# Attention and two mixture layers on one core: a weight guard by magnitude and floor, column steps with pointer scalars, and a new order of all operations

## The chip, the cores and the metric

The kernel runs on one core of a Trainium2 chip. Its time is the device time of one execution in microseconds (us), the median over several executions. A core has five engines that matter here: TensorE (PE, matrix products, with a separate weight load PEld), VectorE (DVE), ScalarE (ACT), GpSimd (POOL) and the queue engine SyncE (SP), which issues the DMA transfers. Each engine works through its own list of instructions in a fixed order and waits, on semaphores, for what an instruction needs.

## The reference

Three layers follow each other. Only the shapes matter for the time, and the 64-bit weights of the second layer, which are the subject of the change.

```python
# 1. attention: B=4 batches, H=8 heads, 512 local + 32 global positions, head size 64
s_ll = where(|i - j| <= 32, scale * q_l @ k_l.T, -1e9)      # local: a band
a_l  = softmax(concat([scale * q_l @ k_g.T, s_ll]))          # and all global keys
out_l = a_l @ concat([v_g, v_l]);  out_g = softmax(scale * q_g @ k_all.T) @ v_all
# 2. x: 2304 tokens x 512.  w_in 512 x 1024 and w_out 1024 x 512 are scaled in NumPy
#    by a float64 scalar and so come in as 64-bit floats
h = x @ w_in;  solu = h * softmax(h)
ln = (solu - mean) / sqrt(var + 1e-6) * g_ln;   x2 = ln @ w_out
# 3. soft mixture of 8 experts with 4 slots each
logits = x2 @ phi;  slot_in = softmax(logits, axis=0).T @ x2
slot_out[e] = relu(slot_in[e] @ w1[e]) @ w2[e];  out = softmax(logits, axis=1) @ slot_out
```

## The kernel before

**Attention.** Tokens are worked on in 16 local tiles of 128 and in 4 global tiles. A local tile has matrix products of queries and keys (L710), a VectorE step that adds the mask and takes the row maximum (L718, output tile `E`), exponentials on ScalarE (L723), transposes on TensorE (L740), copies (L742), products with v (L755), a scaling on VectorE (L762) and a VectorE transpose (L766) into `xp`, the input tile of the next layer. The global tiles have the same steps on other lines: maxima at L795 to L798, sums and reciprocal at L809 and L810.

**Second layer.** There are 17 dense tiles. Each needs its input split into a high part (ScalarE, L859) and a low part (GpSimd subtraction, L860), and then takes 24 matrix products of 128x128 by 128x512 against the high and low parts of w_in (L868, output `h`; called h products below). Softmax and normalisation follow on VectorE and ScalarE (L883 to L932), with small steps on columns of 128x1: L884 takes the smaller of two negated maxima, L902 and L929 prepare mean and variance. `ln` (L911) goes through TensorE transposes (L921) into the product with w_out, which the kernel folds with phi into a small matrix `pb` (L664 to L682).

**Weights.** The 16 pieces of w_in and w_out (8 each, 128x512 numbers of 64 bits, tile `wst`) come in as pairs of 32-bit words. `load_weight` makes 32-bit floats of them: three integer steps on VectorE (L586 to L588, called bits below) join the words. A guard sets numbers that are too small for the format to zero. It has two forms. Form D (4 pieces of w_in): ScalarE squares the high word read as a float (L589), and VectorE compares and multiplies in one step (L593). Form P (12 pieces): the same square, then a comparison (L598) and a product (L599) on GpSimd. A w_in piece is then split into high (ScalarE, L610) and low (GpSimd, L611) parts.

**Third layer.** 47 units of w1 and w2 are loaded into slots as they come free; their products are at L1102 and L1143, and the combination and the stores follow at L1153 to L1180.

**What sets the order.** All operations are collected in a list, with an engine, an estimated duration and a priority each. `Schedule.run` walks a simulated time: whenever an engine is free it takes the ready operation with the lowest priority number, if the operation's buffers fit under the limits `CAPS` and `KEEP` for each kind of buffer (four `wst` buffers, for instance). The table `PRIORITY` has one number for each operation that is added to its priority. The result is a fixed order for each engine and for the DMA issues of SP (L533).

Of the kernel before, what the change touches and what calls it, by code (L numbers as in the profile page):

```python
# [103 lines left out]
class Fetch:  # L104
# [11 lines left out]
    def run(self, o, t, d):  # L116
        room = self.BLOCK - self.n % self.BLOCK
        if o.count >= room:
            self.entered = t + d * room / o.count
# [4 lines left out]
class Schedule:
# [40 lines left out]
    def run(self, on_start=None):  # L165
# [74 lines left out]
        while done < n:  # L240
            progress = False
            waits = []
            for e in engines:
# [115 lines left out]
CAPS = dict(h=10, p1=20, E=15, W=23, eT=29, lT=13, ln=15, q=17, u=9, v=25, wst=4, xhl=5, xp=3)  # L359
KEEP = dict(p1=3, E=3, W=2, eT=2, eg=6, lT=1, ln=5, mkx=22, q=1, u=3, v=7, w=10, wo=14, wst=3, xhl=4)  # L360
# [10 lines left out]
STAY = 16.0807791841  # L371
# [987 lines left out]
```

## Time and profile before

| what | value |
|---|---|
| time, median of 3 runs | 307.65 us (305.86 to 309.4) |
| profiled execution, own time | 306.45 us |
| its span in the trace | 304.7 us (1.75 us lie outside) |
| PE busy | 275.2 us (90%) |
| DVE busy | 203.8 us (67%) |
| ACT busy | 200.1 us (66%) |
| POOL busy | 112.8 us (37%) |
| moved by DMA | 73.0 MB, mean 240 GB/s |
| chain that ended last, by engine | PE 71%, DVE 11%, DMA 9%, ACT 4% |

Busy time is an average over the span, so the table alone does not say which engine decides at which time; a table by stretches of time does. The chain that ended last is found by going back from the last instruction to what released it, step by step.

### The profile page before, as it was taken

How to read it: one execution, taken by the hardware profiler on the slowest of the kernel's cores; microseconds unless marked ns; L12 is line 12 of the kernel's file. 1: busy time of each engine (PE TensorE's matmuls, PEld its weight loads, DVE VectorE, ACT ScalarE, POOL GpSimd, SP SyncE). 2: the span in 40 equal slices, each digit the busy share in tenths (PEclk: the TensorE clock that was granted, in tenths of full speed). 3: DMA queues.
4: the chain of work that ended last, by engine and by line, in shares of the span. 5: the costliest groups of instructions: out<-in, count | busy, mean ns of one | idle time of the engine just before them, and what ended most of it. 6: DMA issues, size and time to landing. Idle time of an engine off the chain costs nothing.

```text
span 304.7 us, 10894 instructions
## 1 busy us (share of the span) xinstructions
PE 275.2 (90%) x4374; PEld 205.6 (67%) x4374; DVE 203.8 (67%) x752; ACT 200.1 (66%) x655; POOL 112.8 (37%) x179
## 2 busy tenths in 40 slices
PE   1576888999999999999999999999999999998980
PEld 1455566786777887777788878877778775364660
DVE  0789899999997578967786777458577861020350
ACT  1766958798789699896898696557467772010250
POOL 0257759897663234243112253224231572000000
PEclk9999999999999999999999999999999999999996
DMA  6999999984202202398649408638545986999498
GB/s 209 407 404 413 409 409 404 408 334 134 86 2 74 71 12 71 81 400 303 230 142 356 137 2 306 225 94 267 197 162 198 339 291 212 357 375 360 132 307 266
DMA packets 31090, 72.99 MB, mean 240 GB/s; under 512 B 2624, under 2 KB 13376, under 8 KB 30656
## 3 DMA queue, kind: packets, MB, share of 16 engines
q1 hardware_dynamic: 30848, 72.17, 65.8%
q8 instruction: 34, 0.56, 0.8%
q10 hardware_dynamic: 192, 0.13, 0.2%
q14 instruction: 16, 0.13, 0.1%
HBM read 67.83 MB, written 4.46 MB: 237 GB/s over the span
## 4 chain that ended last, share of the span: by engine, by line
PE 71%; DVE 11%; DMA 9%; ACT 4%; SPq 2%; issue 2%; DVEq 0%; ACTq 0%
PE h L868 27%; PE p L921 5%; PE p L710 4%; PE p L1102 4%; PE p L755 4%; DMA v<-in_v 4%; PE p L740 4%; PE p L1143 3%; PE p L942 3%; DMA unit<-in_w 3%; PE p L987 3%; DMA q<-in_q 2%; PE p L831 2%; PE p L788 2%; SPq L533 2%
## 5 line engine op out<-in xcount | busy, mean ns | idle before, releaser
L868 PE MATMUL h<-w,xhl 128*128 128x512 f32 x408 | 106.1, 404 | 0.0
L868 PEld LDWEIGHTS h<-w,xhl 128*128 128x128 f32 x408 | 73.0, 189 | 15.7 <-issue 1.3
L723 ACT ACTIVATE E<-E,nmx 128x128 f32<-128x128 f32 x128 | 49.7, 393 | 8.9 <-DVE nmx L718 8.8
L718 DVE CUSTOM_DVE_ANT_0 E<-p,mkx 128x128 f32<-128x128 f32 x128 | 29.2, 284 | 8.6 <-PE p L710 8.2
L889 ACT ACTIVATE u<-h,st 128x512 f32<-128x512 f32 x34 | 23.2, 688 | 13.6 <-DVE st L884 13.6
L710 PE MATMUL p<-k,q 64*32 64x128 f32 x1024 | 22.3, 309 | 8.2 <-DMA q<-in_q 7.6
L883 DVE TENSOR_REDUCE st<-h 128x1 f32<-128x512 f32 x34 | 22.8, 683 | 10.0 <-PE h L868 9.7
L740 PE MATMUL p<-cs,E 128*128 128x128 f32 x128 | 21.9, 306 | 4.7 <-ACT E L723 4.7
L710 PEld LDWEIGHTS p<-k,q 64*32 64x32 f32 x1024 | 17.1, 118 | 13.1 <-DMA k<-in_k 7.9
L892 DVE SCALAR_TENSOR_TENSOR u<-h,u 128x512 f32<-128x512 f32 x34 | 22.9, 682 | 3.3 <-ACT u L889 3.1
L723 ACT ACTIVATION_READ_ACCUMULATOR E<-E,nmx 128x1 f32 x128 | 24.6, 192 | 0.0
L860 POOL TENSOR_TENSOR xhl<-xp,xhl 128x512 fp32r<-128x512 f32 x16 | 20.5, 1284 | 10.3 <-ACT xhl L859 10.1
L755 PE MATMUL p<-v,eT 128*32 128x64 f32 x1024 | 21.1, 234 | 3.2 <-DMA v<-in_v 2.0
L740 PEld LDWEIGHTS p<-cs,E 128*128 128x128 f32 x128 | 16.6, 154 | 9.2 <-ACT E L723 6.7
L755 PEld LDWEIGHTS p<-v,eT 128*32 128x32 f32 x1024 | 17.5, 118 | 7.5 <-issue 3.1
L598 POOL TENSOR_SCALAR wst<-wst 128x512 f32<-128x512 f32 x12 | 19.3, 1605 | 8.8 <-ACT wst L589 8.5
L926 ACT ACTIVATE lT<-p 128x512 f32<-128x512 f32 x33 | 18.8, 601 | 5.4 <-PE p L921 5.3
L742 ACT ACTIVATE eT<-p 128x512 f32<-128x512 f32 x32 | 18.8, 599 | 2.5 <-PE p L740 2.4
L927 ACT ACTIVATE u<-ln 128x1024 f32<-128x1024 f32 x17 | 18.0, 1060 | 3.6 <-DVE ln L911 3.6
L932 POOL TENSOR_TENSOR st<-st,eps 128x1 f32<-128x1 f32 x17 | 9.7, 569 | 25.9 <-DVE st L929 25.7
L921 PE MATMUL p<-cs,ln 128*128 128x128 f32 x136 | 19.1, 276 | 0.0
L728 POOL TENSOR_SCALAR r<-sm 128x8 f32<-128x8 f32 x16 | 4.3, 271 | 34.4 <-ACT E L723 34.0
(140 smaller groups left out, 556.8 us busy)
## 6 DMA issues: line engine op xcount, KB each, us to landing
unit<-in_w SPq DMA_DIRECT2D x47, 512.0 KB, 5.3
v<-in_v SPq DMA_DIRECT2D x28, 512.0 KB, 9.1
k<-in_k SPq DMA_DIRECT2D x3, 1536.0 KB, 8.8
k<-in_w SPq DMA_DIRECT2D x9, 512.0 KB, 5.0
wst<-in_w_out SPq DMA_DIRECT2D x8, 512.0 KB, 10.2
wst<-in_w_in SPq DMA_DIRECT2D x8, 512.0 KB, 10.4
out<-unit SPq DMA_DIRECT2D x8, 512.0 KB, 4.3
unit<-in_w SPq DMA_DIRECT2D x14, 256.0 KB, 7.3
```

The costliest lines, as they stand in the source:

```text
L598: op("Pool", 1680, lambda: nc.gpsimd.tensor_scalar(out=low(), in0=low(), scalar1=least * least, scalar2=None, op0=ALU.is_ge), (), (st,), d ...
L710: nc.tensor.matmul(out=sp[hh][32 * c : 32 * c + 32, a2 + i, :], lhsT=Q[rows, 4 * (a2 + i) + c, :], rhs=K[rows, c, s : s + 128], start=True ...
L718: nc.vector.tensor_tensor_reduce(out=E[:, hh, a, :], in0=sp[hh][:, a, :], in1=MK(mask_kind(4 * t + a)), scale=-SCALE, scalar=3.0e38, op0=A ...
L723: nc.scalar.activation(out=E[:, hh, a, :], in_=E[:, hh, a, :], func=AF.Exp, bias=nmx[:, hh, a : a + 1], scale=-1.0, accum_out=sm[:, hh, a ...
L740: nc.tensor.transpose(out=tp[:, a, :], in_=E[:, hh, a, :], identity=I())
L755: nc.tensor.matmul(out=av[32 * c : 32 * c + 32, hh, a, :], lhsT=eT[hh][:, a, 32 * c : 32 * c + 32], rhs=V[:, (g - 1) % 2, 64 * h : 64 * h ...
L860: op("Pool", 1250, lambda: nc.gpsimd.tensor_tensor(out=xl.ap, in0=X.ap, in1=xh.ap.bitcast(F32), op=ALU.subtract), (X, xh), (xl,))
L868: nc.tensor.matmul(out=hp[n].ap, lhsT=lhs[:, kt, :], rhs=rhs[kt][n].ap, start=(kt == 0 and lhs is xh and rhs is whi), stop=(kt == 3 and lh ...
L883: op("DVE", 602, lambda n=n: nc.vector.tensor_reduce(out=part(7 + n), in_=hp[n].ap, axis=AX.X, op=ALU.max, negate=True), (hp[n],), (col[7 ...
L889: op("ACT", 664, lambda n=n: nc.scalar.activation(out=u[:, n, :], in_=hp[n].ap, func=AF.Exp, bias=nm(), scale=1.0, accum_out=part(7 + n)), ...
L892: op("DVE", 613, lambda n=n: nc.vector.scalar_tensor_tensor(out=u[:, n, :], in0=hp[n].ap, scalar=1.0, in1=u[:, n, :], op0=ALU.mult, op1=AL ...
L921: nc.tensor.transpose(out=tp[:, n, :], in_=ln[:, f // 2, 128 * (f % 2) : 128 * (f % 2) + 128], identity=I())
```

## The change

1. All 16 pieces get one new guard, form M. ScalarE first takes the absolute value of the high word, read as a float, into the destination (L608 in the changed kernel). GpSimd takes the larger of that and a constant floor, in place (L609). Then the three bits steps run on VectorE (L598 to L600 in the changed kernel); the first of them now reads the floored word. The ScalarE and GpSimd steps therefore stand ahead of the bits, where the square, comparison and product stood behind them.
2. Four kinds of VectorE steps on columns are written as `tensor_scalar` with a column as pointer scalar, in place of two tensor inputs: the two steps L797 and L798 become one, and L809, L884 and L929 change their form.
3. The planner gets new constants (latency after a load, a delay behind slot-limited loads, a rule that keeps two marked GpSimd and VectorE operations apart), new limits `CAPS` and `KEEP`, and a new `PRIORITY` table, so the order of every engine is new. Line numbers move by 10 to 12.

```diff
-        def bits(last):
+        def bits(last, words):
             w = d.ap.bitcast(I32)
-            nc.vector.tensor_scalar(out=w, in0=st[:, :, 1], scalar1=3, scalar2=0x3FFFFFFF, op0=ALU.logical_shift_left, op1=ALU.bitwise_and)
+            nc.vector.tensor_scalar(out=w, in0=words, scalar1=3, scalar2=0x3FFFFFFF, op0=ALU.logical_shift_left, op1=ALU.bitwise_and)
...
-            op("DVE", 2050, lambda: bits(dst), (st,), (d, dst), dp=dp)
-            square()
-            op("Pool", 1680, lambda: nc.gpsimd.tensor_scalar(out=low(), in0=low(), scalar1=least * least, scalar2=None, op0=ALU.is_ge), (), (st,), dp=dp)
-            op("Pool", 1395, lambda: nc.gpsimd.tensor_tensor(out=dst.ap, in0=dst.ap, in1=low(), op=ALU.mult), (st,), (dst,), dp=dp)
+            op("ACT", 587, lambda: nc.scalar.activation(out=dst.ap, in_=high(), func=AF.Abs), (st,), (dst,), dp=dp)
+            op("Pool", 1680, lambda: nc.gpsimd.tensor_scalar(out=dst.ap, in0=dst.ap, scalar1=below, scalar2=None, op0=ALU.max), (), (dst,), dp=dp)
+            op("DVE", 2050, lambda: bits(dst, dst.ap.bitcast(I32)), (st,), (d, dst), dp=dp)
...
-                nc.vector.tensor_tensor(out=st[:, 2:3], in0=st[:, 0:1], in1=st[:, 1:2], op=ALU.max)
-                nc.vector.tensor_scalar(out=st[:, 2:3], in0=st[:, 2:3], scalar1=-SCALE, scalar2=None, op0=ALU.mult)
+                nc.vector.tensor_scalar(out=st[:, 2:3], in0=st[:, 0:1], scalar1=st[:, 1:2], scalar2=-SCALE, op0=ALU.max, op1=ALU.mult)
...
-                nc.vector.scalar_tensor_tensor(out=st[:, 5:6], in0=st[:, 3:4], scalar=1e-9, in1=st[:, 4:5], op0=ALU.add, op1=ALU.add)
+                nc.vector.tensor_scalar(out=st[:, 5:6], in0=st[:, 3:4], scalar1=1e-9, scalar2=st[:, 4:5], op0=ALU.add, op1=ALU.add)
...
-        op("DVE", 76, lambda: nc.vector.tensor_tensor(out=nm(), in0=part(7), in1=part(8), op=ALU.min), (col[7], col[8]), (col[0],))
+        op("DVE", 76, lambda: nc.vector.tensor_scalar(out=nm(), in0=part(7), scalar1=part(8), scalar2=None, op0=ALU.min), (col[7], col[8]), (col[0],))
...
-GUARD_IN, GUARD_OUT = "DP", "PP"
+GUARD_IN, GUARD_OUT = "MM", "MM"
...
-CAPS = dict(h=10, p1=20, E=15, W=23, eT=29, lT=13, ln=15, q=17, u=9, v=25, wst=4, xhl=5, xp=3)
-KEEP = dict(p1=3, E=3, W=2, eT=2, eg=6, lT=1, ln=5, mkx=22, q=1, u=3, v=7, w=10, wo=14, wst=3, xhl=4)
+CAPS = dict(h=9, p1=48, E=24, W=33, eT=35, lT=13, ln=17, q=8, u=15, v=27, wst=13, xhl=27, xp=17)
+KEEP = dict(p1=1, E=3, W=8, eT=2, lT=1, ln=3, mkx=26, q=3, u=2, v=1, w=7, wo=8, wst=4, xhl=4, xp=1)
...
-STAY = 16.0807791841
+STAY = 0.639248030591
```

**The order at three places.** The first is the start of SP's queue, so the order in which the first transfers are issued. `k` and `q` are keys and queries, `mkx` the mask, `cs` constants, `wst` a weight piece. Before:

```order
L533 DMA cs_70<-in_cst 128x256
L533 DMA k_72<-in_k 128x4x224
L533 DMA q_74<-in_q 128x512
L533 DMA mkx_76<-in_cst 128x512
L533 DMA k_72<-in_k 128x4x192
L533 DMA q_74<-in_q 128x512
L533 DMA wst_115<-in_w_out 128x1024
L533 DMA q_117<-in_q 128x512 x2
L533 DMA v_160<-in_v 128x1024
L533 DMA wst_176<-in_w_in 128x1024
```

In the changed kernel:

```order
L545 DMA mkx_70<-in_cst 128x512
L545 DMA k_72<-in_k 128x4x224
L545 DMA wst_74<-in_w_in 128x1024
L545 DMA q_76<-in_q 128x512
L545 DMA cs_78<-in_cst 128x256
L545 DMA wst_80<-in_w_in 128x1024
L545 DMA k_72<-in_k 128x4x192
L545 DMA wst_86<-in_w_in 128x1024
L545 DMA wst_90<-in_w_in 128x1024
L545 DMA q_76<-in_q 128x512
```

Four pieces of w_in moved ahead of the second query block; before, the first weight piece, one of w_out, stood behind it. All eight w_in pieces are issued within the first 11.9 MB of transfers, where it was 17.2 MB.

The second place is the start of VectorE. `p` is a scratch tile in PSUM, `W` a w_in piece, `E` the masked scores of a local tile. Before, from the end of the first local tile's rows on:

```order
L718 ISA E_82,nmx_120<-p_7_80,mkx_76 128x128
L718 ISA nmx_120 128x1
L586 TENSOR_SCALAR p_18_171<-wst_115 128x512
L587 SCALAR_TENSOR_TENSOR p_18_171<-wst_115,p_18_171 128x512
L588 SCALAR_TENSOR_TENSOR wo_172<-wst_115,p_18_171 128x512
L718 ISA E_125,nmx_191<-p_13_123,mkx_76 128x128
```

In the changed kernel, from the first row behind the clearing of a buffer on:

```order
L598 TENSOR_SCALAR p_13_92<-W_82 128x512
L599 SCALAR_TENSOR_TENSOR p_13_92<-wst_74,p_13_92 128x512
L600 SCALAR_TENSOR_TENSOR W_82<-wst_74,p_13_92 128x512
L598 TENSOR_SCALAR p_19_137<-W_88 128x512
L599 SCALAR_TENSOR_TENSOR p_19_137<-wst_80,p_19_137 128x512
L600 SCALAR_TENSOR_TENSOR W_88<-wst_80,p_19_137 128x512
L729 ISA E_99,nmx_182<-p_15_98,mkx_70 128x128
L729 ISA nmx_182 128x1
```

The bits of two w_in pieces moved ahead of the first local tile's rows (L729 is the old L718).

The third place is TensorE around its first h products. `xhl` is a split input tile, `w` a split piece of w_in. Before:

```order
L755 MATMUL p_89_550<-v_228,eT_434 32x64 x4
L755 MATMUL p_89_550<-v_412,eT_434 32x64 x8
L755 MATMUL p_89_550<-v_401,eT_434 32x64 x4
L868 MATMUL h_571<-w_498,xhl_399 128x512 x3
L868 MATMUL h_571<-w_495,xhl_399 128x512 x3
L740 MATMUL p_96_593<-cs_70,E_459 128x128 x4
```

In the changed kernel:

```order
L721 MATMUL p_63_385<-k_72,q_251 32x128
L721 MATMUL p_64_386<-k_72,q_251 32x128
L878 MATMUL h_69_430<-w_324,xhl_420 128x512 x3
L878 MATMUL h_69_430<-w_141,xhl_420 128x512 x3
L721 MATMUL p_73_457<-k_72,q_251 32x128
L721 MATMUL p_74_458<-k_72,q_251 32x128
```

The first h product moved from row 166 to row 113 of TensorE: it now stands behind the scores of three local tiles, where before it stood behind four and the scores of a global tile.

## Rows read from the trace of the kernel before

**Rows 1.** Busy time by stretches of the span; the columns are named in the second line.

```profile
core 0: us, PE busy (x) PEld busy (x) DVE busy (x) ACT busy (x) POOL busy (x), PEclk, DMA share, GB/s
0.00:10.00 10.00, 2.45 (x88) 2.05 (x96) 2.27 (x16) 2.52 (x8) 0.30 (x5) 1.00 0.77 256
10.00:20.00 10.00, 6.05 (x79) 4.69 (x67) 7.97 (x28) 8.54 (x34) 4.49 (x5) 1.00 1.03 408
20.00:30.00 10.00, 7.02 (x196) 5.41 (x196) 9.38 (x31) 5.88 (x17) 7.29 (x7) 1.00 1.06 407
30.00:40.00 10.00, 8.79 (x155) 6.01 (x159) 8.40 (x31) 9.00 (x36) 6.51 (x7) 1.00 1.01 413
40.00:50.00 10.00, 7.44 (x228) 5.56 (x222) 9.76 (x22) 6.59 (x15) 7.43 (x6) 1.00 1.01 404
50.00:100.00 50.00, 49.56 (x888) 37.24 (x888) 47.09 (x184) 44.12 (x159) 34.03 (x35) 1.00 0.50 185
100.00:256.00 156.00, 155.23 (x2320) 122.96 (x2319) 110.01 (x428) 116.20 (x378) 52.77 (x117) 1.00 0.56 193
256.00:304.70 48.70, 38.65 (x456) 21.68 (x454) 8.95 (x18) 7.28 (x15) 0.00 (x0) 0.94 0.88 302
```

**Rows 2.** Waits of PE: total us, how many times, the longest.

```profile
PE p L710 <- DMA q<-in_q: 7.6, 2, 6.4
PE p L740 <- ACT E L723: 4.7, 2, 2.8
```

**Rows 3.** Timeline of PE, rows apart: start us, us, line, tiles, count.

```profile
9.52 1.96 PE L710 MATMUL p<-k,q 64*32 64x128 f32 x64 [1.20 <-DMA q<-in_q]
...
37.80 1.69 PE L868 MATMUL h<-w,xhl 128*128 128x512 f32 x6
...
50.16 1.17 PE L868 MATMUL h<-w,xhl 128*128 128x512 f32 x4
...
58.28 1.16 PE L710 MATMUL p<-k,q 64*32 64x128 f32 x64
```

**Rows 4.** Lines of the guard: duration min/median/max in ns, first and last start.

```profile
L586 DVE TENSOR_SCALAR p<-wst x16: 668/688/695, 10.7 to 83.2; 128x512 int32<-128x512 int32 x16
L589 ACT ACTIVATE wst<-wst x16: 646/681/728, 13.1 to 85.5; 128x512 f32<-128x512 f32 x16
L593 DVE SCALAR_TENSOR_TENSOR W<-wst,p x4: 669/681/687, 31.4 to 45.2; 128x512 f32<-128x512 f32 x4
L598 POOL TENSOR_SCALAR wst<-wst x12: 1555/1582/1883, 13.8 to 86.3; 128x512 f32<-128x512 f32 x12
L599 POOL TENSOR_TENSOR wo<-wo,wst x8: 1293/1312/1323, 15.4 to 88.3; 128x512 f32<-128x512 f32 x8
L860 POOL TENSOR_TENSOR xhl<-xp,xhl x16: 1268/1284/1313, 27.3 to 192.6; 128x512 fp32r<-128x512 f32 x16
```

**Rows 5.** The same view for VectorE's column steps; L902 already has a pointer scalar.

```profile
L809 DVE SCALAR_TENSOR_TENSOR gst<-gst x8: 141/152/1098, 46.4 to 188.5; 128x1 f32<-128x1 f32 x8
L884 DVE TENSOR_TENSOR st<-st x17: 103/154/1227, 66.5 to 239.3; 128x1 f32<-128x1 f32 x17
L929 DVE SCALAR_TENSOR_TENSOR st<-st x17: 137/159/1150, 79.0 to 245.8; 128x1 f32<-128x1 f32 x17
L902 DVE TENSOR_SCALAR st<-st x17: 158/208/215, 73.1 to 241.8; 128x1 f32<-128x1 f32 x17
```

**Rows 6.** Timelines of DVE and of POOL at the same two moments.

```profile
74.51 1.23 DVE L884 TENSOR_TENSOR st<-st 128x1 f32<-128x1 f32 x1
...
116.14 0.21 DVE L902 TENSOR_SCALAR st<-st 128x1 f32<-128x1 f32 x1
...
74.41 2.56 POOL L860 TENSOR_TENSOR xhl<-xp,xhl 128x512 fp32r<-128x512 f32 x2 [1.02 <-ACT xhl L859]
...
115.45 1.29 POOL L860 TENSOR_TENSOR xhl<-xp,xhl 128x512 fp32r<-128x512 f32 x1
```

**Rows 7.** Timeline of DVE: its first row behind a wait.

```profile
8.43 0.29 DVE L718 CUSTOM_DVE_ANT_0 E<-p,mkx 128x128 f32<-128x128 f32 x1 [6.77 <-PE p L710]
```

**Rows 8.** Timeline of POOL: the last w_in piece gets its low part.

```profile
59.21 1.29 POOL L611 TENSOR_TENSOR w<-W,w 128x512 fp32r<-128x512 f32 x1
```

More of the change, by code (lines that the diff above doesn't have):

```diff
@@ L27 @@
 SCALE = 0.125
+LANDING, BEHIND = 2150, 1200
 LAT = {
@@ L39, in latency @@
 def latency(a, b):
-    return float(LAT.get((a, b), 2000 if a == "SP" else 0))
+    return float(LAT.get((a, b), LANDING if a == "SP" else 0))
 class Region:
@@ L120, in run @@
             self.TIME = 6400.0 if self.entered < 62000 else 5000.0
+            self.n += o.count
+            return True
         self.n += o.count
+        return False
 class Schedule:
@@ L137, in slot, with op @@
         return Buf(self, pool, None, shape, dtype, 1, cls)
-    def op(self, eng, dur, fn, ins=(), outs=(), dp=0.0, touch=(), heat=1.0, tiled=False, count=0):
+    def op(self, eng, dur, fn, ins=(), outs=(), dp=0.0, touch=(), heat=1.0, tiled=False, count=0, port=False):
         o = Op()
+        o.port = int(port)
         o.eng, o.dur, o.fn, o.heat, o.tiled = eng, dur, fn, heat, int(tiled)
@@ L184, in run @@
         cand = {e: [o.idx for o in ops if o.eng == e and not o.deps] for e in engines}
-        efree = {e: 2300.0 if e == "SP" else 0.0 for e in engines}
+        efree = {e: 1900.0 if e == "SP" else 0.0 for e in engines}
         order, events = [], []
@@ L188, in run @@
         t, done = 0.0, 0
+        porting = [-1.0, -1.0]
+        since, fetched = -1.0, -1e9
         def clear(o, t):
@@ L193, in clear @@
                 waits.append(fetch.start(o))
+                return False
+            if o.port and porting[o.eng == "DVE"] > t + 1e-9:
+                waits.append(porting[o.eng == "DVE"])
                 return False
@@ L279, in run @@
                     tiled = o.tiled
-                    fetch.run(o, t, d)
+                    if fetch.run(o, t, d):
+                        fetched = fetch.entered
+                if e == "SP" and t > efree[e] + 1.0:
+                    since = t
+                if o.port:
+                    porting[e == "Pool"] = t + d
                 efree[e] = t + d
@@ L328, in run @@
                     ndep[s] -= 1
-                    ready_t[s] = max(ready_t[s], te + latency(o.eng, ops[s].eng))
+                    ready_t[s] = max(ready_t[s], te + latency(o.eng, ops[s].eng) + (BEHIND if o.eng == "SP" and since - 500.0 < fetched <= te else 0.0))
                     if ndep[s] == 0:
@@ L529, in ps1, with load @@
         return slot("ps", "p1", shape)
-    def load(dst, src, nbytes, view=None, chunk=4096):
+    def load(dst, src, nbytes, view=None, chunk=4096, rate=1.0):
         op("SP", max(nbytes / RATE_DMA if chunk == 4096 else nbytes / 410.0 * (1 + 160.0 / chunk), 430.0), lambda: nc.sync.dma_start(out=dst.ap if view is None else view(dst.ap), in_=src), (), (dst,))
@@ L569, in kernel_body @@
         w_in, w_out = w_in.bitcast(I32), w_out.bitcast(I32)
-    least = float(np.array(LEAST_HI, np.int32).view(np.float32))
+    least, below = (float(np.array(x, np.int32).view(np.float32)) for x in (LEAST_HI, LEAST_HI - (1 << 20)))
     def load_weight(src, dst, guard, dp):
@@ L590, in load_weight @@
         if guard == "D":
-            op("DVE", 2050, lambda: bits(d), (st,), (d,), dp=dp)
+            op("DVE", 2050, lambda: bits(d, st[:, :, 1]), (st,), (d,), dp=dp)
             square()
@@ L610, in load_w_in @@
         op("ACT", 520, lambda: nc.scalar.activation(out=hi.ap, in_=w.ap, func=AF.Copy), (w,), (hi,), dp=PWIN)
-        op("Pool", 1225, lambda: nc.gpsimd.tensor_tensor(out=lo.ap, in0=w.ap, in1=hi.ap.bitcast(F32), op=ALU.subtract), (hi, w), (lo,), dp=PWIN)
+        op("Pool", 1225, lambda: nc.gpsimd.tensor_tensor(out=lo.ap, in0=w.ap, in1=hi.ap.bitcast(F32), op=ALU.subtract), (hi, w), (lo,), dp=PWIN, port=True)
     def load_w_out(i):
@@ L859, in dense_tile @@
         op("ACT", 520, lambda: nc.scalar.activation(out=xh.ap, in_=X.ap, func=AF.Copy), (X,), (xh,))
-        op("Pool", 1250, lambda: nc.gpsimd.tensor_tensor(out=xl.ap, in0=X.ap, in1=xh.ap.bitcast(F32), op=ALU.subtract), (X, xh), (xl,))
+        op("Pool", 1250, lambda: nc.gpsimd.tensor_tensor(out=xl.ap, in0=X.ap, in1=xh.ap.bitcast(F32), op=ALU.subtract), (X, xh), (xl,), port=True)
         hp = [slot("ps", "h2" if j >= J0 and (j - J0) % 2 == 1 else "h", [128, 512]) for n in range(2)]
@@ L908, in dense_tile @@
                 op("DVE", 396, lambda n=n: nc.vector.tensor_scalar(out=ln[:, 2 * n : 2 * n + 2, :], in0=u[:, n, :].rearrange("p (q f) -> p q f", q=2),
-                                                                   scalar1=mean(), scalar2=None, op0=ALU.add), (ur[n], col[5]), (cens[n],))
+                                                                   scalar1=mean(), scalar2=None, op0=ALU.add), (ur[n], col[5]), (cens[n],), port=True)
         else:
-            op("DVE", 668, lambda: nc.vector.tensor_scalar(out=ln.ap, in0=flat(), scalar1=mean(), scalar2=None, op0=ALU.add), (*ur, col[5]), (cen,))
+            op("DVE", 668, lambda: nc.vector.tensor_scalar(out=ln.ap, in0=flat(), scalar1=mean(), scalar2=None, op0=ALU.add), (*ur, col[5]), (cen,), port=True)
         stage(f"T{j}")
@@ L927, in dense_tile @@
         op("ACT", 1040, lambda: nc.scalar.activation(out=flat(), in_=ln.ap, func=AF.Square, accum_out=ssq()), (*cens, lT[0]) if last else (cen,), (*ur, col[3]))
-        op("DVE", 70, lambda: nc.vector.scalar_tensor_tensor(out=qq(), in0=ssq(), scalar=1.0 / DF, in1=qq(), op0=ALU.mult, op1=ALU.add), (col[3],), (col[4],))
+        op("DVE", 70, lambda: nc.vector.tensor_scalar(out=qq(), in0=ssq(), scalar1=1.0 / DF, scalar2=qq(), op0=ALU.mult, op1=ALU.add), (col[3],), (col[4],))
         def powers():
@@ L1191, in tail @@
                 if j0 < 16:
-                    op("SP", max((1.25 * w + 25.0) * group, 430), lambda store=store: store(nc.sync), obr, ())
+                    op("SP", max((1.45 * w + 25.0) * group, 430), lambda store=store: store(nc.sync), obr, ())
                 else:
```

2 lines of the change are left out of this document (1 added, 1 removed), and 205 rows, old and new, of the table PRIORITY.

## The prediction

> **What bounds the kernel now.** I read the busy time by stretches first [rows 1], since a mean over the span hides the stages. From 50 to 256 us TensorE is busy 49.56 + 155.23 = 204.79 of 206 us: there it is the bound, and whatever makes another engine faster can win at most 1.2 us. The time that TensorE loses lies elsewhere. In the first 50 us it is idle for 7.55 + 3.95 + 2.98 + 1.21 + 2.56 = 18.25 us, and in the last 48.7 us for 10.05 us. Its own work in the first stretch is dear as well: 64 products of L710 take 1.96 us at 9.5 us and 1.16 us at 58 us [rows 3], although the granted clock reads 1.00 in both stretches [rows 1]. So the same work costs 1.7 times as much while TensorE is fed poorly.
>
> Then the waits. The longest of TensorE are for the first queries, 7.6 us, and for exponentials, 4.7 us [rows 2]; both belong to the start. VectorE is nearly full from 20 to 50 us, with 9.38, 8.40 and 9.76 of each 10 us, and the DMA share is about 1.0 from 10 to 50 us [rows 1]. What TensorE lacks there is the h products, 24 for each tile and the bulk of its work. The first six come at 37.8 us, more from 50.2 us on [rows 3], since they need split pieces of w_in, and the last of those is made at 59.21 + 1.29 = 60.5 us [rows 8]. So the change can win where it brings h products forward: before 50 us. It can lose in the same place.
>
> **The guard, GpSimd's part.** The comparison takes 1.58 us and the product 1.31 us [rows 4], 12 of each. In their place stand 16 maxima. No maximum of 128x512 is in the trace. The nearest rows are the comparison, also with one tensor and a constant but on every second word, 1.58 us, and a two-tensor subtraction on dense words, 1.28 us (L860) [rows 4]. I take 1.4 us and keep 1.28 and 1.6 as ends. Up to the low part of the last w_in piece, GpSimd's list holds 7 comparisons, 6 products and 12 subtractions before: 11.1 + 7.9 + 15.4 = 34.4 us. After, it holds 10 maxima and 10 subtractions: 12.8 to 16 plus 12.8, so 25.6 to 28.8 us. That is 6 to 9 us less. Its first row is a maximum, which needs the first weight piece and an absolute value (like the square, 0.68 us [rows 4]). Before the second weight piece 2.15 MB are issued with it; at the 256 GB/s of the first 10 us [rows 1] it has landed at 8.4 us, and with a landing delay about 9.5. So GpSimd works from about 9 us on. If it never waits it has the last w_in piece done at 35 to 38 us; with the 26.1 us that it spends on other things before 60.5 in the trace (60.5 - 34.4) it is 52 to 55. The truth lies between. I walked its rows one by one against their inputs and came to 41.5 to 44.4, and take 43: 17 us earlier than now.
>
> The Trainium skill, page "GPSIMD Engine Reference", section 3.1, counts about 1.8 cycles for each element with one input and 2.6 with two. For 512 elements it gives 0.77 us; by that estimate the ten maxima cost 7.7 us and not 14. The trace's one-input step at 1.58 us, slower than the two-input ones, doesn't bear that out. By the row and by the page alike TensorE's time below changes only where GpSimd is what it waits for.
>
> **The guard, VectorE's and ScalarE's part.** The four L593 go: 4 x 0.68 = 2.7 us, at 31.4 to 45.2 us [rows 4], where VectorE is full. The 16 bits keep their three steps; the first reads dense words and I leave it at 0.69 us. ScalarE's 16 squares become 16 absolute values, cost nothing more and change no count. What is added is a wait: bits now stand behind ScalarE and GpSimd, where before they started on the transfer alone. VectorE's list begins with the bits of two pieces, and the local tiles' rows queue behind them. Absolute value at 9.5, two maxima one after the other (the first can run while the second piece lands), two hand-overs, and three bits steps of 0.69 each end at about 15 us. The first local row then stands at 15 us and not at 8.43 [rows 7].
>
> **The columns.** L884 takes 154 ns in the middle but 1227 at worst, L929 159 and 1150, L809 152 and 1098 [rows 5]. The worst ones lie beside GpSimd work: the 1.23 us at 74.51 beside two subtractions from 74.41 on, so it ended with the first of them [rows 6]. The pointer form L902 never took more than 215 ns, also at 116.14 beside a subtraction that ran from 115.45 to 116.74 [rows 5, 6]. So the new forms cost up to 208 ns and don't wait. Over the 17 + 17 + 8 columns this adds at most 42 x 0.055 = 2.3 us. The three worst waits take away 0.95 + 1.07 + 0.99 = 3.0 us [rows 5], and the eight steps saved at L797 and L798 some 8 x 0.15 = 1.2 us at the price of their kind. The net is 2 us of VectorE. All but the 0.95 of L809 at 46.4 lie after 50 us, under a TensorE that is 99% busy, so I price the columns at 0 there, and at 0.95 us within the gain below. Were TensorE not the bound there, up to 2 us would be theirs.
>
> **The order.** (a) The first h products need the split input of the first tile. From the first local row to that took 8.43 to 27.3 + 1.28 = 28.6 us before [rows 4, 7], 20.2 us with waits for v among them. From 15 us on it is 35 at the latest, and about 29 if v and ScalarE, no longer crowded by the squares and w_out, are ready. I take 29, which is 8.8 us before 37.8 [rows 3]. TensorE was idle for 6.75 us from 20 to 50 us [rows 1]; I take half as filled, **+3.4** (0 to 6.7). (b) It leaves the dear stretch earlier. Work there costs 1 - 1.16/1.96 = 41% too much [rows 3]; 8.8 us at 85% busy would give 3.0; I take **+2.5** (0 to 3). (c) The first q now stands behind a weight piece and the mask: 1.5 MB to its end and not 0.85, so 0.65 MB at 408 GB/s [rows 1], **-1.6**. (d) Exponentials of the first tile come 6.6 us later; what TensorE did in that time (scores of further tiles) fills part; its wait for them, 4.7 us in all [rows 2], grows. I take **-1.0** (0 to -5). The sum is +3.3 us, with the ends at +8.1 and -6.6.
>
> Behind 50 us: TensorE's rows are as many in every kind (1,276 and 1,274 rows in the order), so 0 (-1 to +1). The tail: from its start on 26 transfers of 9.7 MB remain in both orders, into slots that come free through TensorE's products, so the loads move along: 0 (-1.5 to +1.5).
>
> 306.45 us of the profiled execution less 3.3 gives 303.2. The median of the three runs is 1.2 us above that execution, and on its scale it is 304.4. I say 303.5.
>
> **The rivals.** *The start eats the gain* (slower). Bits wait for ScalarE and GpSimd, and all local rows stand behind. Each us by which the first local row comes later than 15 us is a us for TensorE, as long as it has nothing else to do, until h products flow. At 19 us the gain is 3.3 - 4 = -0.7; at 22 us it is -3.7, some 310.5. It decides at 18.3 us. For it: the DMA is full from 10 us on [rows 1], and three engines take turns. Against it: here the pieces stand third and sixth in the queue.
>
> *Given back.* The front wins 3 us, but TensorE then runs out of tiles between 50 and 100 us, since VectorE's work there, 47.09 of 50 us [rows 1], gets lighter only by the columns; or the tail's loads come no sooner, as DMA is 0.88 full there [rows 1]. Then about 306.5. Against it: its four L593 are gone before, 2.7 us [rows 4], so its queue reaches 50 us further on.
>
> *All of it works.* First h at 28 us, idle time from 20 to 50 us gone: +6.7 + 3.0 - 1.6 = 8.1, so 298.5 to 299.5.
>
> *The pointer forms wait all the same.* Then VectorE keeps 3.0 us of waits, and the front loses its 0.95: 304.5. The Trainium skill, page "SBUF — State Buffer", section "Who interferes with whom", lets a VectorE step with two SBUF inputs contend with GpSimd, and a `tensor_scalar` too if it enters a two-port mode. By the latter rule L911, 0.73 us for 1024 elements, contends, and the new forms could. For columns, L902 speaks against it with its 215 ns [rows 5].
>
> **How the numbers follow.** Forecast 0.43 (301 to 306), given back 0.22, all works 0.15, start eats it 0.16, forms wait 0.04. About 1% (3 us) is what a measurement of this kernel tells from no change. Against 307.65, faster by over 1% is below 304.6: 0.32 of the forecast, 0.15 of the best case, and 0.05 of the others, so 0.52. Slower, above 310.7, are 0.13 of the start rival and 0.02 for a stall of the new order that I don't see, so 0.15. The same is 0.33. The range must hold eight in ten: it leaves out 0.05 of the best case and the 0.15 above, which gives 298.8 to 308.5; the forecast's own range is 301 to 306.
>
> **What would show it.** In the profile after: the first local row of VectorE at 15 us (if it is 18 or later the start rival holds); first h product at 29 and the last low part of w_in at 43; TensorE's busy time from 20 to 50 us up from 23.25 and the same 99% from 50 to 256; no column step above 0.3 us; the maximum between 1.28 and 1.6 us; the tail from the first L1102 product on as long as now. The prediction is wrong if the maxima make GpSimd the bound to 50 us, or if TensorE's idle time moves behind 50 us.

## The result, and the profile after

| | before | after |
|---|---|---|
| median | 307.61 us (305.86 to 309.4, 4 runs) | 301.98 us (301.0 to 302.29, 4 runs) |
| ratio to before, 95% interval | | 0.984 (0.981 to 0.988) |
| span of the profiled execution | 304.7 us | 299.0 us |
| PE / DVE / ACT / POOL busy | 275.2 / 203.8 / 200.1 / 112.8 us | 271.9 / 197.6 / 199.7 / 102.2 us |

The changed kernel is 1.6% faster, 5.6 us where 303.5 us (4.1 us less than the median of before) was forecast; 301.98 lies inside the range. The table of busy time by stretches of the profile after answers to [rows 1]; its columns are the same.

```profile
0.00:10.00 10.00, 0.00 (x0) 0.00 (x0) 0.70 (x1) 1.94 (x2) 0.94 (x6) 1.00 0.78 255
10.00:20.00 10.00, 5.89 (x134) 4.10 (x134) 8.37 (x40) 7.10 (x26) 7.77 (x6) 1.00 1.03 406
20.00:30.00 10.00, 9.41 (x208) 6.71 (x208) 9.55 (x23) 8.50 (x26) 6.92 (x7) 1.00 1.05 408
30.00:40.00 10.00, 8.13 (x154) 5.68 (x155) 9.37 (x35) 9.68 (x38) 9.64 (x9) 1.00 1.01 397
40.00:50.00 10.00, 10.00 (x193) 7.55 (x192) 9.86 (x50) 9.70 (x41) 7.08 (x8) 1.00 1.03 406
50.00:100.00 50.00, 49.40 (x896) 37.17 (x894) 39.69 (x145) 40.04 (x135) 16.55 (x23) 1.00 0.62 210
100.00:256.00 156.00, 154.75 (x2381) 120.48 (x2376) 111.08 (x433) 115.50 (x381) 53.28 (x117) 1.00 0.56 196
```

TensorE starts later and does nothing in the first 10 us, but from 20 to 50 us it is busy 27.54 us and not 23.25. The next rows are of the timelines of DVE, of PE and of POOL after (start, duration, line); they answer to [rows 7], [rows 3] and [rows 8].

```profile
10.90 0.69 DVE L598 TENSOR_SCALAR p<-W 128x512 int32<-128x512 int32 x1 [9.24 <-POOL W L609]
...
15.30 0.28 DVE L729 CUSTOM_DVE_ANT_0 E<-p,mkx 128x128 f32<-128x128 f32 x1
...
29.02 0.73 PE L878 MATMUL h<-w,xhl 128*128 128x512 f32 x2
...
41.83 1.29 POOL L622 TENSOR_TENSOR w<-W,w 128x512 fp32r<-128x512 f32 x1
```

The first local row stands at 15.3 us, the first h product at 29.0 us, and the last w_in piece has its low part at 43.1 us. The waits of PE after answer to [rows 2].

```profile
PE p L721 <- DMA k<-in_k: 12.2, 1, 12.2
PE p L751 <- ACT E L734: 1.0, 1, 1.0
```

The lines of the new guard and of the column steps, by line with minimum, median and maximum in ns, answer to [rows 4] and [rows 5].

```profile
L609 POOL TENSOR_SCALAR W<-W x8: 1479/1486/1512, 9.4 to 36.1; 128x512 f32<-128x512 f32 x8
L819 DVE TENSOR_SCALAR gst<-gst x8: 203/213/215, 74.9 to 190.2; 128x1 f32<-128x1 f32 x8
L894 DVE TENSOR_SCALAR st<-st x17: 195/207/215, 47.5 to 235.7; 128x1 f32<-128x1 f32 x17
L939 DVE TENSOR_SCALAR st<-st x17: 173/210/215, 68.3 to 241.7; 128x1 f32<-128x1 f32 x17
```

No column step waits any more: the longest of all takes 0.216 us. Last, the line of the first w1 products, with which the tail begins; first before, then after.

```profile
L1102 PE MATMUL p<-unit,lps x108: 592/592/617, 256.2 to 269.7; 128*32 128x512 f32 x108
```

```profile
L1112 PE MATMUL p<-unit,lps x120: 592/592/617, 252.6 to 266.0; 128*32 128x512 f32 x120
```

Up to there 3.6 us are won (256.2 - 252.6). From there to the end of the span it is 48.5 us before and 46.4 after: 2.1 us more.

### The profile page after: what moved, and what is told of

Read it like the earlier page. It is cut to its first block, busy times and chain, and to the rows that moved or that the text cites. A ratio compares the mean times of both kernels' runs of the same rounds, so it can differ in the third digit from the quotient of the medians.

```text
span 299.0 us, 10878 instructions
## 1 busy us (share of the span) xinstructions
PE 271.9 (91%) x4374; PEld 200.8 (67%) x4374; DVE 197.6 (66%) x740; ACT 199.7 (67%) x655; POOL 102.2 (34%) x171
## 4 chain that ended last, share of the span: by engine, by line
PE 70%; DVE 13%; DMA 8%; ACT 3%; issue 2%; POOL 1%; SPq 1%; ACTq 0%; DVEq 0%
PE h L878 27%; PE p L931 5%; DMA unit<-in_w 5%; PE p L766 5%; PE p L751 4%; PE p L721 4%; PE p L997 3%; PE p L952 3%; PE p L1153 3%; DMA wst<-in_w_in 2%; PE p L841 2%; DVE p L599 2%; PE p L1112 2%; DVE p L598 2%; PE p L830 2%
## 5 line engine op out<-in xcount | busy, mean ns | idle before, releaser
L878 PE MATMUL h<-w,xhl 128*128 128x512 f32 x408 | 107.8, 406 | 2.1 <-POOL w L622 1.0
L729 DVE CUSTOM_DVE_ANT_0 E<-p,mkx 128x128 f32<-128x128 f32 x128 | 28.9, 285 | 5.2 <-PE p L721 5.0
L721 PE MATMUL p<-k,q 64*32 64x128 f32 x1024 | 19.8, 291 | 13.4 <-DMA k<-in_k 12.2
L721 PEld LDWEIGHTS p<-k,q 64*32 64x32 f32 x1024 | 15.7, 112 | 17.7 <-issue 13.6
L902 DVE SCALAR_TENSOR_TENSOR u<-h,u 128x512 f32<-128x512 f32 x34 | 22.7, 684 | 2.2 <-ACT u L899 2.0
L766 PE MATMUL p<-v,eT 128*32 128x64 f32 x1024 | 20.0, 232 | 1.1 <-issue 0.6
L931 PE MATMUL p<-cs,ln 128*128 128x128 f32 x136 | 20.5, 278 | 0.4 <-DVE ln L918 0.4
L751 PEld LDWEIGHTS p<-cs,E 128*128 128x128 f32 x128 | 15.2, 148 | 5.7 <-ACT E L734 4.3
L753 ACT ACTIVATE eT<-p 128x512 f32<-128x512 f32 x32 | 18.0, 596 | 0.6 <-PE p L751 0.5
L931 PEld LDWEIGHTS p<-cs,ln 128*128 128x128 f32 x136 | 15.4, 141 | 4.0 <-issue 1.4
L906 POOL TENSOR_SCALAR st<-st 128x1 f32<-128x1 f32 x17 | 5.7, 338 | 30.2 <-ACT u L899 25.6
```

What stands on the lines that cost most here:

```text
L721: nc.tensor.matmul(out=sp[hh][32 * c : 32 * c + 32, a2 + i, :], lhsT=Q[rows, 4 * (a2 + i) + c, :], rhs=K[rows, c, s : s + 128], start=True ...
L729: nc.vector.tensor_tensor_reduce(out=E[:, hh, a, :], in0=sp[hh][:, a, :], in1=MK(mask_kind(4 * t + a)), scale=-SCALE, scalar=3.0e38, op0=A ...
L751: nc.tensor.transpose(out=tp[:, a, :], in_=E[:, hh, a, :], identity=I())
L766: nc.tensor.matmul(out=av[32 * c : 32 * c + 32, hh, a, :], lhsT=eT[hh][:, a, 32 * c : 32 * c + 32], rhs=V[:, (g - 1) % 2, 64 * h : 64 * h ...
L878: nc.tensor.matmul(out=hp[n].ap, lhsT=lhs[:, kt, :], rhs=rhs[kt][n].ap, start=(kt == 0 and lhs is xh and rhs is whi), stop=(kt == 3 and lh ...
L902: op("DVE", 613, lambda n=n: nc.vector.scalar_tensor_tensor(out=u[:, n, :], in0=hp[n].ap, scalar=1.0, in1=u[:, n, :], op0=ALU.mult, op1=AL ...
```

## The experiments

Ratios are to the kernel before, run on the same chip beside each kernel, with the 95% interval. "Tail start" is the first w1 product in the profiled execution. In all variants of the changed kernel the order of every engine is kept unless it is said otherwise.

| kernel | median us | ratio | tail start | from there to the end |
|---|---|---|---|---|
| before | 306.6 to 307.6 | 1 | 256.2 | 48.5 |
| after | 301.98 | 0.984 (0.981 to 0.988) | 252.6 | 46.4 |
| after, old columns | 301.78 | 0.986 (0.981 to 0.990) | 252.9 | 46.8 |
| before, new columns | 303.21 | 0.989 (0.985 to 0.993) | 252.5 | 48.1 |
| before, new guard in 12 pieces | 311.65 | 1.020 (1.013 to 1.027) | 260.1 | 49.0 |
| after, 2.07 us of VectorE at 13 us | 302.49 | 0.988 (0.982 to 0.993) | 253.7 | 47.2 |
| after, 2.07 us of VectorE at 60 us | 304.0 | 0.992 (0.989 to 0.995) | 255.3 | 46.1 |
| before, 2.07 us of VectorE at 61 us | 309.45 | 1.010 (1.006 to 1.013) | 260.5 | 48.8 |
| after, every maximum twice | 316.63 | 1.032 (1.025 to 1.039) | 268.2 | 47.0 |
| after, half a local tile first | 301.06 | 0.983 (0.978 to 0.988) | 252.8 | 46.5 |

**Old columns in the changed kernel.** The four changes of form are undone, in this manner, and nothing else:

```diff
-        op("DVE", 76, lambda: nc.vector.tensor_scalar(out=nm(), in0=part(7), scalar1=part(8), scalar2=None, op0=ALU.min), ...
+        op("DVE", 76, lambda: nc.vector.tensor_tensor(out=nm(), in0=part(7), in1=part(8), op=ALU.min), ...
```

> The changed kernel with its order kept row for row, and only the column steps written as before (two ops for the maximum of the global tiles, two-tensor forms for the other three). Theory 'start and order' (the gain was made before 50 us, and TensorE covers VectorE behind it): the columns wait for GpSimd again, some 3 us of VectorE in all, and the time stays at 302 to 302.8 us. Rival 'columns' (the waits were on the path): 304 to 305 us.

Measured: 301.78 us, a ratio of 0.986 beside 0.984. The old forms cost nothing that can be seen here. But they also hardly wait. The only one of the four that waits at all is the maximum of the global tiles, three times, from 144 us on, 0.82 us at worst:

```profile
L808 DVE TENSOR_TENSOR gst<-gst x8: 159/160/819, 71.2 to 185.4; 128x1 f32<-128x1 f32 x8
```

The timelines of DVE and POOL of this run show the difference between two kinds of neighbour:

```profile
183.68 0.82 DVE L808 TENSOR_TENSOR gst<-gst 128x1 f32<-128x1 f32 x1
...
46.77 0.16 DVE L895 TENSOR_TENSOR st<-st 128x1 f32<-128x1 f32 x1
```

```profile
183.18 2.55 POOL L871 TENSOR_TENSOR xhl<-xp,xhl 128x512 fp32r<-128x512 f32 x2 [3.06 <-ACT xhl L870]
...
44.54 2.95 POOL L609 TENSOR_SCALAR wo<-wo 128x512 f32<-128x512 f32 x2 [0.32 <-ACT wo L608]
```

Beside a subtraction with two tensors the column takes 0.82 us. Beside two maxima, which have one tensor and a constant, the same form takes 0.16 us. The new guard has no product with two tensors, so it takes away a neighbour that the old columns would have waited for. That is part of it: in the kernel before, two of the long waits lie beside such products (0.88 us at 81.23, 1.15 us at 88.49) and two beside subtractions (1.10 us at 46.38, 1.23 us at 74.51), which the changed kernel still has. Up to 140 us its order lets no old column wait for one.

**New columns in the kernel before.** The same four changes, alone, in the old order.

> The kernel before with its order kept and only the column steps in the new form. Theory 'start and order': 306.6 to 307.6 us, since only the one at 46 us (1.10 us) lies before 50 us. Rival 'columns': 304 to 305 us.

Measured: 303.21 us beside 306.57, 3.4 us less. That is the rival's number, and more than half of the whole result comes back from this part alone. The line of L884 (one line earlier in this run) no longer shows a wait:

```profile
L883 DVE TENSOR_SCALAR st<-st x17: 161/206/215, 64.9 to 235.5; 128x1 f32<-128x1 f32 x17
```

Busy time by stretches, of this run:

```profile
50.00:100.00 50.00, 49.95 (x898) 38.71 (x896) 44.35 (x178) 45.01 (x164) 34.53 (x37) 1.00 0.53 193
```

TensorE's busy time from 50 to 100 us went up by only 0.39 us, from 49.56 [rows 1]. Counting h products in that stretch gives 97 before and 102 here, though, and 12 and 19 before 50 us. The tail starts 3.7 us earlier. The order is the same, so TensorE can be compared row by row. In this execution it is 0.8 us ahead by 20 us, where no column stands yet, then 1.9 at 50, 1.6 at 77 and 3.5 at 96 us. Most of the 1.0 us won by 50 us is this wait, which is 0.33 us here:

```profile
49.88 0.52 PE L820 MATMUL p<-cs,eg 128*128 128x128 f32 x3 [1.24 <-DVE wo L588]
```

The 1.9 us from 77 to 96 us lie where hardly any idle time is shown before. They lie inside groups of rows that take longer, as these six small products, first before, then here:

```profile
89.71 1.36 PE L664 MATMUL p<-cs,wo 128*128 128x128 f32 x6
```

```profile
87.03 0.82 PE L664 MATMUL p<-cs,wo 128*128 128x128 f32 x6
```

One such row is 0.27 us long, but undisturbed the next starts 0.11 us after it (0.82 us for six). So a stop of up to some 0.16 us between two rows, an estimate from these figures, leaves no gap and counts as busy. The busy share did not show what could be won.

**New guard in the kernel before.** The 12 pieces of form P get the new guard. The absolute value and the maximum are placed some 3 us ahead of the bits; where the transfer had only just landed, the bits move back by up to 3 us.

```diff
-            op("DVE", 2050, lambda: bits(dst), (st,), (d, dst), dp=dp)
-            square()
-            op("Pool", 1680, ... op0=ALU.is_ge ...)
-            op("Pool", 1395, ... op=ALU.mult ...)
+            op("DVE", 2050, lambda: bits(dst, dst.ap.bitcast(I32)), (st,), (d, dst), dp=dp)
+            op("ACT", 587, ... func=AF.Abs ...)
+            op("Pool", 1680, ... op0=ALU.max ...)
...
+        key[i + 1], key[i + 2], key[i] = (abs_at, -1), (abs_at + 700, -1), (bits_at, -1)
```

> The kernel before with its order kept, but the 12 pieces of form P in the new guard: absolute value and maximum placed some 3 us ahead of the bits, the bits up to 3 us later where the transfer had only just landed. The 4 pieces of form D stay. GpSimd gets some 17 us lighter. Theory 'start and order' (the guard alone brings no h product forward, since TensorE's rows stand where they stood): 306 to 309 us. Rival 'guard' (GpSimd's relief is what counts): 303 to 305 us.

Measured: 311.65 us, 5.1 us slower, outside both numbers. Two waits show what the guard costs in an order that wasn't made for it (waits of DVE in the first 100 us):

```profile
DVE p L587 <- POOL W L599: 2.0, 2, 1.3
DVE p L587 <- POOL wo L599: 1.0, 2, 0.5
```

And busy time by stretches:

```profile
20.00:30.00 10.00, 4.66 (x196) 3.63 (x194) 9.27 (x32) 5.58 (x14) 4.71 (x4) 0.92 1.05 407
30.00:40.00 10.00, 7.84 (x139) 5.43 (x140) 8.27 (x33) 10.00 (x39) 6.34 (x7) 0.67 1.01 412
```

From 20 to 30 us TensorE does as many products as before, 196, in 4.66 us and not 7.02 [rows 1], so that is no loss by itself. But it stands 4.03 us for exponentials, where it stood 1.89 before, and behind that its products are dear again: 64 of L712 took 1.15 us at 25.06 and take 1.96 at 32.56.

```profile
30.23 2.40 PE L742 MATMUL p<-cs,E 128*128 128x128 f32 x8 [4.03 <-ACT E L725]
```

Its granted clock is 0.67 from 30 to 40 us, so between its two levels of 1.2 and 2.4 GHz, where it was 1.00 before. GpSimd's relief is there (22.8 us from 50 to 100 us, not 34.0), and it wins nothing in this order. How much of the 5.1 us is the guard's and how much the places that I chose for it this run doesn't tell.

**VectorE delayed, at the start and at 60 us.** One first bits step runs four times, 2.07 us more. Once it is the second piece, once the 14th, and in the kernel before the 13th.

```diff
-            nc.vector.tensor_scalar(out=w, in0=words, ...
+            for _ in range(again("DVE", {2: 4})):
+                nc.vector.tensor_scalar(out=w, in0=words, ...
```

> The changed kernel, same order, with the first bits step of the second weight piece run four times and not once: 3 x 0.69 = 2.07 us more of VectorE right ahead of the first local tile's rows, at about 13 us. If each us at the start is a us at the end, as the start rival of the prediction has it: 303.8 to 304.3 us, and TensorE is 2 us further behind by 50 us. If another engine or the loads bound the first 50 us, 302 to 302.6 us.

> The changed kernel, same order, with the same 2.07 us of VectorE put in at the 14th piece, at about 60 us, where VectorE is 98% busy and TensorE 97 to 98%. Theory of the prediction (TensorE covers VectorE behind 50 us): 302 to 302.4 us. Rival (TensorE's busy share hides that it waits; VectorE still sets the pace there): 303.3 to 304.1 us.

> The kernel before, same order, with the same 2.07 us of VectorE put in at the 13th piece, at about 61 us. The run with new columns took 3.4 us off the kernel before by taking some 4 us of waits from VectorE between 36 and 89 us. If VectorE sets the pace there: 308 to 308.7 us. If TensorE covers it: 306.5 to 307 us, and the gain of the new columns has another cause.

Measured: 302.49, 304.0 and 309.45 us. At the start the ratio rises by 0.0033, about 1.0 us, and the tail starts 1.1 us later: half of what the start rival asked for, and the intervals overlap. At 60 us it rises by 0.0074 in the changed kernel and by 0.0096 in the kernel before, 2.3 and 2.9 us: all of it, and a little more. What TensorE does at 60 us in the changed kernel with the delay (without it, it is busy for 9.76 us there, at a granted clock of 1.00):

```profile
60.00:70.00 10.00, 7.41 (x94) 4.91 (x93) 9.79 (x18) 4.30 (x13) 2.77 (x2) 0.83 0.21 68
```

Part of the loss is then the clock's. The delayed bits end at 62.82 + 0.69 = 63.51 us, and only then does TensorE go on, after 2.33 us:

```profile
62.82 0.69 DVE L607 SCALAR_TENSOR_TENSOR wo<-wst,p 128x512 int32<-128x512 int32 x1
63.61 1.08 PE L776 MATMUL p<-v,eT 128*32 128x64 f32 x32 [2.33 <-issue]
```

In the kernel before with the delay, TensorE is 1.3 us late already ahead of the delay (its granted clock is 0.73 from 30 to 40 us in this execution), and 4.1 us late behind it, so 2.8 us are the delay's. Its waits behind the delay; without it, 55 to 90 us has none of this size:

```profile
67.16 0.63 PE L747 MATMUL p<-cs,E 128*128 128x128 f32 x4 [0.79 <-DVE wo L595]
...
68.43 0.63 PE L747 MATMUL p<-cs,E 128*128 128x128 f32 x4 [0.64 <-DVE nmx L725]
...
72.91 0.65 PE L762 MATMUL p<-v,eT 128*32 128x64 f32 x32 [0.94 <-DVE wo L595]
```

TensorE was 99% busy there and yet had no reserve against VectorE. The reason is in the rows. The products that wait for the bits don't read `wo`, which the third bits step writes; they write a scratch tile `p`. The program has 8 tiles in PSUM for all scratch tiles and `h`, and the bits hold one of them until their third step has read it. By the program's order the tile of the delayed piece goes next to L776 in the changed kernel and to L747 in the kernel before, and that of the piece behind it there to L762. When the bits are late, the product waits for its tile, and everything behind it in TensorE's list waits too. The wait of L820 above is of the same kind: a column that took 1.10 us at 46.38 us held up the bits behind it, and L820 needed their tile.

**Every maximum twice.** GpSimd gets 16 x 1.49 = 24 us more, in the new order. For a piece that is the load of the old guard (2.98 us and 2.89), but for 16 pieces, where the old guard had 12 on GpSimd: 48 us in all and not 35.

```diff
-            op("Pool", 1680, lambda: nc.gpsimd.tensor_scalar(out=dst.ap, in0=dst.ap, scalar1=below, ...
+            def floor():
+                for _ in range(2):
+                    nc.gpsimd.tensor_scalar(out=dst.ap, in0=dst.ap, scalar1=below, ...
```

> The changed kernel, same order, with every maximum on GpSimd run twice: 16 x 1.49 = 24 us more, which gives the guard the GpSimd time of the form before (2.9 us for a piece). GpSimd is busy for 34 of the first 43 us here. If GpSimd's relief is what lets the order start its h products early, the last w_in piece is done at about 53 us and the time is 306 to 309 us; if GpSimd has room, below 303 us.

Measured: 316.63 us, 14.6 us slower than the changed kernel. The line of the low parts, and the waits of PE:

```profile
L632 POOL TENSOR_TENSOR w<-W,w x8: 1268/1272/1285, 21.4 to 52.4; 128x512 fp32r<-128x512 f32 x8
```

```profile
PE h L888 <- POOL xhl L880: 4.4, 2, 3.7
PE h L888 <- POOL w L632: 4.1, 2, 2.6
```

The last w_in piece is done at 53.7 us, as expected. The loss is larger than the 306 to 309 that I gave, as GpSimd's split of the input tiles is late too. So the new order has no room for this load on GpSimd. Whether it has room for that of the old guard, 13 us less, was not run.

**Half a local tile first.** One query block is loaded ahead of the first weight piece, and 8 of the first 16 local rows run before the bits.

```diff
+    first = [133, 132, 3, 0, 8, 30, 29, 4, 36, 134, 135, 136, 31, 32, 1, 78, 137, ...]
+    order = first + [i for i in order if i not in set(first)]
```

> The changed kernel with another start by hand: one query block is loaded ahead of the first weight piece, and half of the first local tile's VectorE rows (8 of 16) run ahead of the bits, in the time in which VectorE waits for the first piece. All behind keeps its order. If VectorE bounds the first 50 us, the 1.7 us of work that moves into idle time is won: 300.4 to 301 us. If the weights or TensorE bound it, the weight pieces come 0.65 us later: 302 to 302.8 us.

Measured: 301.06 us, ratio 0.983 beside 0.984. Local rows start at 8.81 us and not at 15.30, and the tail at 252.8 beside 252.6. So filling the idle time of VectorE in the first 10 us is worth nothing that shows, and the start isn't bound by VectorE alone. But the weights come later here (first bits at 12.21 us and not 10.90), so the run has a gain and a loss in one. It is the lowest median here, but it can't be told from the changed kernel.

**Bits in SBUF.** The word that the three steps pass on lies in a PSUM scratch tile. In SBUF the first step has the form in which L921 does two elements in the time of one.

```diff
-            w = d.ap.bitcast(I32)
+            w = (last if own else d).ap.bitcast(I32)
```

> The changed kernel, same order, but for the 8 pieces of w_out the bits steps keep their word in the piece's own tile in SBUF and not in a PSUM scratch tile. The first step then is one tensor and constants from SBUF to SBUF, the form in which L921 does 1024 elements in 0.75 us, so it should take about 0.42 and not 0.69 us. Seven of the eight lie before 70 us, where 2.07 us more of VectorE cost 2 us. If VectorE sets the pace there: 1.5 to 2 us less than the changed kernel, 300 to 300.6 us. If the second and third step, now with two SBUF tensors, wait for GpSimd, as the columns did before: 302 to 304 us.

> The same for all 16 pieces. The w_in pieces lie before 40 us, where GpSimd is full with maxima and two-tensor subtractions (doubling its maxima cost 14.6 us). If the first step's gain of 0.27 us for a piece counts more: 298.5 to 300 us. If the steps with two SBUF tensors wait for the subtractions, and GpSimd waits for them: slower than with the 8 pieces, 302 to 305 us.

> The 8 pieces of w_out in SBUF together with the start of the run in which half of the first local tile goes ahead of the bits. That start took 0.5 us off, within its interval of no change. If the two add up: 299.5 to 300.3 us; if the second is nothing: the time of the run with 8 pieces.

Measured: 302.78 us with the 8 pieces of w_out (ratio 0.988, 0.983 to 0.993), 306.95 with all 16 (1.003, 0.9995 to 1.005), and 302.26 with the 8 pieces and the other start (0.987, 0.982 to 0.992). The first step does fall from 0.69 to 0.42 us, but then waits. By line, of the run with 16 pieces:

```profile
L598 DVE TENSOR_SCALAR W<-W x8: 416/427/1491, 9.6 to 41.2; 128x512 int32<-128x512 int32 x8
L599 DVE SCALAR_TENSOR_TENSOR W<-wst,W x8: 691/836/1662, 10.1 to 42.2; 128x512 int32<-128x512 int32 x8
L609 POOL TENSOR_SCALAR W<-W x8: 1478/1732/1933, 8.1 to 38.3; 128x512 f32<-128x512 f32 x8
```

Both sides lose: the steps wait up to 1.66 us, and the maxima take up to 1.93 us and not 1.49. VectorE's gain of 0.27 us for a piece is paid back, so keeping the word in PSUM is no worse. (The scratch tile stays reserved in these runs; what giving it free would be worth was not tried.)

## Why the prediction was right, and where it was not

**The start, as walked through.** The instants held closely: first local row 15 (15.3), first h product 29 (29.0), last w_in piece 43 (43.1), maximum 1.4 us between 1.28 and 1.6 (1.49), columns below 0.3 us (0.216 at most), TensorE's busy time from 20 to 50 us up (27.54). The estimate of 0.77 us for the maximum, from what the Trainium skill, page "GPSIMD Engine Reference", section 3.1, gives as the best case, was half of the 1.49 us that it takes.

**Terms (a) to (d).** The sum of +3.3 us fits the 3.6 us by which the tail starts earlier. The terms did not all hold. TensorE's idle time from 20 to 50 us fell from 6.75 to 2.46 us, so (a) was 4.3 and not 3.4. Term (b) held in kind: the dear stretch ends earlier, as 64 products that still take 1.96 us at 31.80 before (first row) take 1.16 at 27.89 after.

```profile
31.80 1.96 PE L710 MATMUL p<-k,q 64*32 64x128 f32 x64
```

```profile
27.89 1.16 PE L721 MATMUL p<-k,q 64*32 64x128 f32 x64
```

What it is worth no run measures by itself. TensorE's busy time up to the tail fell by 2.6 us, but in the run with new columns alone it fell by 2.7, so that time holds hidden waits as well. Term (c) was too small: the first products need the second block of keys, which the term leaves out, and start at 12.24 us and not 6.35. Term (d) had the wrong sign: the wait for exponentials fell from 4.7 to 1.0 us, as TensorE reaches those products later too (17.28 us, not 11.41). Together (c) and (d) were -2.6, and TensorE's idle time in the first 20 us grew by 2.6 us (11.50 to 14.11): that the sum came out there is luck. And the start rival's price, a us for a us, was too high: 2.07 us cost about 1.0.

**Columns at 0 behind 50 us: wrong.** The step that failed is "All but the 0.95 of L809 at 46.4 lie after 50 us, under a TensorE that is 99% busy, so I price the columns at 0 there". 2.07 us of VectorE at 60 us cost 2.3 and 2.9 us, and the new columns alone took 3.4 us off the kernel before. In the profiled execution 0.9 us of that came with L809 (at L820), which the step has at 0.95, and 1.9 us between 77 and 96 us, which it has at 0. Its 3.0 us of waits also left out a long one, the 0.88 us of L884 at 81.23. A busy share of 99% hides short stops, and it says nothing of what a later scratch tile would do to TensorE's list. The first reading, "whatever makes another engine faster can win at most 1.2 us", fails with it.

**So there are two ways to the same sum.** The forecast had the order as the source and the columns beside it. For the change as a whole the runs bear that out: guard and order with old columns keep all of it (301.78 us). But new columns in the old order come to about the same tail start (252.5 us, and 252.9 with guard and order alone). All three together give 252.6, so they don't add up. The column waits of the kernel before, 4.1 us from 36 to 89 us, are gone either way: the new form doesn't wait, and in the new order the old form doesn't up to 140 us. How much of the order's gain is this, and how much the earlier h products, no run separates. From 144 us on old columns wait 1.4 us in the changed kernel, and it doesn't show in the time. That VectorE has room there isn't shown. At 124 us in the same run it had none: a step that takes 0.75 us alone took 1.86, and TensorE then stood 0.97 us.

```profile
124.09 1.86 DVE L922 TENSOR_SCALAR ln<-u,st 128x1024 f32<-128x1024 f32 x1
...
127.54 1.10 PE L766 MATMUL p<-v,eT 128*32 128x64 f32 x64 [0.97 <-DVE lps L958]
```

**The guard.** That it takes the load off GpSimd held, 102.2 us and not 112.8 in all. The new order has no room for 24 us more on GpSimd (14.6 us slower), and the guard is worth nothing in the old one (5.1 us slower in the places that I gave it). The new order with the old guard was not run, so that each needs the other is likely and not shown.

**The tail: "0 (-1.5 to +1.5)" was too small.** From the tail's start to the end it takes 48.1 to 49.0 us in the four runs with the old order and 46.1 to 47.2 in the six with the new one, 1.9 us less in the mean. The order makes it, then, not columns or guard. TensorE's wait there for a weight load is 0.9 us before and 0.3 after, and up to 1.8 in the other eight. Without this wait the tail takes 47.1 to 47.6 us in the four and 46.0 to 46.2 in the six, so the loads make up some 0.7 us of the 1.9 and their scatter. For the other 1.2 the cause is open: two of the eight large stores are issued from 282.95 us on, between the small ones, but that this counts was not tried.

**What stays open.** What the order gives by itself, as said. And the other bounds of the first 50 us: neither 6.5 us of earlier local rows nor 2.07 us of later ones moved the end in full, while GpSimd's load did. Most likely weights and GpSimd set the pace up to 40 us and VectorE behind that; the runs don't place the border.

## What to carry to other kernels

A busy share of 99% is no cover. Before a saving on another engine is priced at 0, look for what in the busy engine's list waits for that engine, be it data or a buffer that it must give free, and put 2 us of extra work there: that one run tells whether the cover exists at that place. This guard, which stands ahead of the bits, lost in an order that wasn't made for it, so try a new form and its order together, and each alone.

## What the runs showed of the hardware that I had not expected

How much VectorE waits for GpSimd depends on the kind of both instructions. A column with two tensors took 1.23 us beside a two-tensor subtraction [rows 6], and 0.16 us beside a maximum with one tensor. A 128x512 step with two SBUF tensors, 0.69 us alone, lies between: timelines of DVE and POOL in the run with 8 pieces in SBUF show it beside a maximum and beside a subtraction.

```profile
49.84 0.98 DVE L600 SCALAR_TENSOR_TENSOR wo<-wst,wo 128x512 int32<-128x512 int32 x1
...
65.62 1.64 DVE L600 SCALAR_TENSOR_TENSOR wo<-wst,wo 128x512 int32<-128x512 int32 x1
```

```profile
49.66 1.51 POOL L609 TENSOR_SCALAR wo<-wo 128x512 f32<-128x512 f32 x1 [0.35 <-ACT wo L608]
...
65.30 1.41 POOL L870 TENSOR_TENSOR xhl<-xp,xhl 128x512 fp32r<-128x512 f32 x1 [1.22 <-ACT xhl L869]
```

The step beside the maximum took 0.98 us and ended before it, at 50.82 and not 51.17, so it wasn't held for the whole instruction; the one beside the subtraction ended at 67.26, after the subtraction at 66.71. The Trainium skill, page "SBUF — State Buffer", section "Who interferes with whom", says that a VectorE step with two SBUF inputs contends with a GpSimd instruction that reads SBUF, and that the loser of such a contention blocks fully. For subtractions these rows agree. For the maximum, which reads SBUF as well, they don't: 0.29 us were added, and nothing to a column.

The pointer form is free of this only for columns. L911, with pointer scalars and 128x1024 elements, takes 0.75 us in the middle, but 1.63 at 212.29 us in the kernel before, beside a subtraction from 212.08 on, and L922 above took 1.86 beside one from 124.11 on. The prediction's remark that L911 contends, and that columns don't, holds.
